# A chunked state-space scan feeding a GELU feed-forward: a new written-out order of all steps, with some steps joined and one mask given a second form

## The chip, the cores and the metric

The kernel runs on one core of one Trainium2 chip. The metric is the device time of one execution in microseconds (us). Three timed executions of the kernel before took 120.58, 120.76 and 121.44 us, so its median is 120.76 us. A further execution was recorded by the hardware profiler; all rows that are quoted come from it.

A core has five engines with a queue each: TensorE (PE; its loads of stationary operands are shown apart as PEld), VectorE (DVE), ScalarE (ACT), GpSimd (POOL) and SyncE (SP, which here only issues transfers). Each engine works through its own queue in the order in which the program issued the instructions, and waits where an operand is not ready.

## What is computed

The reference, cut to what matters. Four batches of eight heads go through a scan in chunks; its result, 3072 tokens of 256, goes through two matrices with a GELU between them.

```python
log_a = np.log(np.clip(a, 1e-06, 1.0))            # x (4,8,768,32), a (4,8,768), B and C (4,8,768,16)
for c in range(nc):
    cum = np.cumsum(la, axis=-1)
    L = np.exp(cum[:, :, :, None] - cum[:, :, None, :]) * causal
    M = np.einsum('bhin,bhjn->bhij', Cc, Bc) * L
    y_intra = np.einsum('bhij,bhjd->bhid', M, xc)
    y_inter = np.einsum('bhin,bhnd->bhid', Cc, state) * np.exp(cum)[:, :, :, None]
    y[:, :, sl] = y_intra + y_inter
    Bx = np.einsum('bhjn,bhjd->bhjnd', Bc, xc) * decay_from_j[:, :, :, None, None]
    state = decay_full[:, :, None, None] * state + np.sum(Bx, axis=2)
x = y.transpose(0, 2, 1, 3).reshape(3072, 256)
h = x @ w_in                                      # 256 x 2048
g = 0.5 * h * (1.0 + np.tanh(c * (h + 0.044715 * h * h * h)))
out = g @ w_out                                   # 2048 x 256
```

## The kernel before, in words

**Tiling.** The kernel uses chunks of 128 time steps, 6 per batch, 24 in all. Two neighbouring chunks are a unit `u`, so there are 12 units of 256 tokens. The eight heads lie side by side on the 128 partitions (16 states each) or in eight groups of 32 columns.

**A list of steps.** The program is cut into named steps (`add`, L722), each a function `f_...` or `c_...` with an engine, the steps it depends on, and the buffers it takes. The string `ORDERED` (L17) names each step once, and the last loop (L895) calls them in that order; so the string alone sets the order of instructions in each engine's queue. A letter behind a colon puts a step on another of the engines that it allows (`:A` ACT, `:D` DVE, `:P` POOL, `:S` SP). `~60` issues 60 blocks of 128 columns of filler matmuls on zeros (`fill`, L672, up to four blocks to an instruction), and `+5` behind an s1 step issues 5 such blocks ahead of it. The tile framework adds the waits that the data demands; it doesn't reorder.

**The scan of a unit.** The steps that the text names are these:

- `load_aq`, `load_a`, `load_bc0`, `load_bc1`, `load_x4`, `load_x`, `load_bc`, `load_wi`, `load_wo`: transfers. `aq` is what the first four chunks need of `a`, `a` is everything of it in two halves. `bc0` brings B (`.0`) and C (`.1`) of chunks 0 to 3 of batch 0, `bc1` of chunks 4 and 5. `x4` is x of chunks 0 to 3. `wi` and `wo` are four blocks each of the two matrices.
- `c_ident`, `c_tri`, `c_cz`, `c_bmask`, `c_m8`: constants made on POOL. `c_bmask` (L232) makes the mask that keeps each head's own block, out of a memset and two affine selects. `c_par` reads it.
- `clipq`, `Rq`, `tpq`, `recip0`: decays of chunks 0 to 3 on DVE; `clip` (L325), `R` (the long scan at L328), `tp2`, `recip1`, `tp6`, `recip`, `pe`: those of all others. `tp2` and `tp6` are transposes on DVE (L339).
- `mulb`, `mulc`, `mul1`, `mul`: B and C times decays on DVE. `tw`, `T1`, `T`: their transposes on PE into PSUM. `ew`, `bh1`, `ce1`, `E`, `F`: the copies out to `bh` and `ce`. `N1`, `N` transpose `bh` back, `bn1`, `bn` copy that out.
- `XX`, `XD`, `xn`: x of the first two units, re-ordered on PE with the products for their states. `castx` does it for later units by a cast.
- `G` (Gram): C times B for both chunks of a unit on PE, in rows of 32, into the PSUM tiles `ga` and `gb`. `M.u.0` and `M.u.1` mask them on DVE (1.2 us each). In unit 0, `GE` and `ME` do half of this by ACT and POOL.
- `D`: the unit's products for the state, on PE, into one of the two PSUM buffers named `hp`. `S` adds them to the state, `SP` makes the masked state for the next chunk; both are on DVE.
- `Y`: the output of both chunks on PE into the PSUM tile `yb`, out of `M`, x and `SP`. `yev` copies it to `xm`.

**The feed-forward of a unit.** `s1.u.i` (L688, eight per unit) multiplies `xm` with two blocks of `w_in` into an `hp` buffer; `gelu.u.i` on ACT (L692) takes it out into `gT`. `s2.u.k.q` (L706) multiplies `gT` with `w_out`, `oev` copies the result out and `store` writes it. `wi.q.k` and `wo.q.k` cast the matrices to bf16 after their loads, on POOL, ACT or DVE. There are two `hp` buffers, shared by `s1`, `D` and a few early steps, and one each of `ga`, `gb` and the output bank.

**The order around the start, before.** On DVE: ... `mulb`, `mulc.0`, `mulc.1`, `peq`, `clip`, two copies, `c_par`, `R`, `M.0.0`, `SP.0`, `S.0.0`, `tp2`, `S.0.1`, `recip1`, `S.1.0`, `mul1.1`, `SP.1`, `M.1.1`, `M.1.0`. On PE: fillers, `tw.0`, `tw.1`, `tw.2`, `G.0`, `XX.0`, `XD.0`, eleven blocks of filler, `Y.0`, `XX.1`, `XD.1`, `s1.0.0`, `G.1` and so on. From unit 3 on the order before has, on PE, `D.3 G.4`, `D.4 Y.3`, `Y.4 D.5 G.5`, `G.6 D.6 Y.5 D.7`, `G.7 D.8 Y.6`, `Y.7 G.8`, `G.9 Y.8 D.9`, `G.10 D.10 Y.9`, `D.11 Y.10 G.11` and `Y.11`, each between s1 and s2 steps.

Of the kernel before, what the change touches and what calls it, by code (L numbers as in the profile page):

```python
# [30 lines left out]
castx.3.None load_x.4 T.1.0 s1.2.1 E.1.0 load_bc.2.1 s2.0.0.2.o E.1.1:A s1.2.2 gelu.2.1 N.1 F.1
castx.4.None gelu.2.2 bn.1:D wo.3.1:D load_bc.2.0 s2.0.1.2.o load_x.5 s1.2.3 wo.3.0:A G.3 M.3.0
s1.2.4 load_bc.3.1 gelu.2.3 load_x.6 s1.2.5 gelu.2.4 s2.0.0.3.o gelu.2.5 s1.2.6 s2.0.1.3.o
gelu.2.6 load_x.7 M.3.1 s1.2.7 D.3 oev.1 S.3.0 oev.0 G.4 gelu.2.7 SP.6 S.3.1 s2.1.0.0.o D.4
castx.7.None Y.3 s2.1.0.1.o s2.1.0.2.o yev.3.0.2 s2.1.0.3.o s1.3.0 S.4.0 M.4.0 S.4.1 M.4.1 mul.2.1
oev.2 s1.3.1 mul.2.0 gelu.3.0 s2.1.1.0.o s2.1.1.1.o gelu.3.1 s1.3.2 load_bc.3.0 s2.1.1.2.o
s2.1.1.3.o gelu.3.2 T.2.1 s1.3.3 SP.8 T.2.0 gelu.3.3 s1.3.4 oev.3:D load_x.8 castx.5.None:A E.2.0
s2.2.0.0.o SP.9 s2.2.0.1.o gelu.3.4 s1.3.5 N.2 s1.3.6 bn.2 E.2.1 s2.2.0.2.o SP.7 gelu.3.5 gelu.3.6
s2.2.0.3.o Y.4 castx.6.None:D yev.4.0.2 D.5 oev.4:D G.5 S.5.0 store.2 s1.3.7 s1.4.0 gelu.3.7
gelu.4.0 s2.2.1.0.o s1.4.1 gelu.4.1 s2.2.1.1.o M.5.0 SP.10 s2.2.1.2.o s1.4.2 s2.2.1.3.o s1.4.3  # L40
gelu.4.2 s1.4.4 M.5.1 gelu.4.3 F.2 G.6 oev.5:D D.6 S.6.0 Y.5 gelu.4.4 S.6.1 D.7 S.7.0 s2.3.0.0.o
# [24 lines left out]
store.19 s2.10.1.0.o s2.11.0.0.yb s1.11.5 s2.10.1.1.o s2.11.0.1.yb store.16 gelu.11.5 s1.11.6  # L66
s2.10.1.2.o gelu.11.6 store.20 s1.11.7 store.15 store.18 s2.10.1.3.o gelu.11.7 oev.21 s2.11.0.2.yb
store.21 s2.11.0.3.yb s2.11.1.0.o s2.11.1.1.o s2.11.1.2.o s2.11.1.3.o oev.22 store.22 oev.23
store.23
# [864 lines left out]
```

## Time and profile before

| what | value |
|---|---|
| timed executions | 120.58, 120.76, 121.44 us |
| the profiled execution | 121.85 us, of which 120.1 us from its first to its last instruction |
| mean granted clock of PE | 0.971 of full speed |
| PE busy | 113.1 us, 94% of the span |
| DVE busy | 74.5 us, 62% |
| ACT busy | 73.0 us, 61% |
| POOL busy | 16.2 us, 14% |
| moved by DMA | 14.00 MB |
| s1 matmuls (L688), 384 | 54.7 us, 277 ns each |
| s2 matmuls (L706), 352 and 32 | 47.4 and 4.5 us, 273 ns each |
| GELU (L692), 96 | 54.2 us, 597 ns each |

A matmul's 277 ns are its length from start to end; neighbours overlap, and four of them start within 0.437 us at the full clock. The page shows the span in 40 slices of 3 us with the busy share of each engine in tenths. "PEclk" is the clock that PE was granted. In rows of the timeline the numbers are the start, the length (of a whole group, if it stands for several instructions), the engine, the line, the operation, what is written and read, the shape and the number; in brackets stands how long the engine was idle just before and what ended that.

Chain of waits that ended last, shares of the span: PE 87%, DMA 7%, ACT 2%, DVE 1%.

### The profile page before, as it was taken

The numbers are of one execution on the slowest core, as the hardware profiler recorded it, in microseconds if no ns is written. First come the engines' busy times: TensorE is split into PE (matmuls) and PEld (weight loads), VectorE is DVE, ScalarE is ACT, GpSimd is POOL, SyncE is SP. The second block draws the span as 40 slices with busy tenths as digits, with TensorE's granted clock in tenths as the row PEclk, the third lists the DMA queues.
The fourth block names the chain that finished last, engine by engine and source line by source line (L and its number), as shares of the span: only waits on it lengthen the run. The fifth ranks groups of instructions, "written<-read, shape, count | busy, mean of one in ns | idle before, by whom it ended". The sixth has DMA issues, their size and how long they took to land.

```text
span 120.1 us, 3430 instructions
## 1 busy us (share of the span) xinstructions
PE 113.1 (94%) x1456; PEld 94.1 (78%) x1456; DVE 74.5 (62%) x147; ACT 73.0 (61%) x142; POOL 16.2 (14%) x33
## 2 busy tenths in 40 slices
PE   6948999999999999999999999999999999999990
PEld 2324457888887998989799979888989899999970
DVE  6289799999979977969597356798645003102000
ACT  2227649966974658668665574543786565576430
POOL 7315776205300020020000000000000000000000
PEclk9997559999999999999999999999999999999999
DMA  3999989996949877900400060006100001001521
GB/s 70 223 294 278 371 216 270 359 247 102 271 76 215 174 136 159 196 8 0 132 5 0 0 124 13 5 6 212 49 27 17 0 5 44 0 5 46 175 87 44
DMA packets 37662, 14.00 MB, mean 117 GB/s; under 512 B 31824, under 2 KB 36112, under 8 KB 37648
## 3 DMA queue, kind: packets, MB, share of 16 engines
q1 hardware_dynamic: 37456, 13.70, 44.5%
q8 instruction: 11, 0.18, 0.6%
q10 hardware_dynamic: 192, 0.10, 0.4%
q14 instruction: 3, 0.02, 0.1%
HBM read 10.65 MB, written 3.15 MB: 115 GB/s over the span
## 4 chain that ended last, share of the span: by engine, by line
PE 87%; DMA 7%; ACT 2%; DVE 1%; issue 0%; ACTq 0%
PE hp L688 36%; PE o_ps L706 32%; DMA a_t<-in_a_dram 5%; PE ga L574 3%; PE yb L706 3%; PE yb L629 3%; PE yb L638 2%; DMA aq_t<-in_a_dram 2%; ACT gT L692 1%; PE yb L676 1%; PE hp L607 1%; PE ga L500 1%; PE gb L481 1%; PE ga L481 1%; PE hp L542 1%; DVE bh L315 1%
## 5 line engine op out<-in xcount | busy, mean ns | idle before, releaser
L692 ACT ACTIVATE gT<-hp 128x512 bf16<-128x512 f32 x96 | 54.2, 597 | 28.0 <-PE hp L688 27.6
L688 PE MATMUL hp<-xm,w_in_sb 128*128 128x256 bf16 x384 | 54.7, 277 | 0.2 <-ACT gT L692 0.2
L706 PE MATMUL o_ps<-w_out_sb,gT 128*128 128x256 bf16 x352 | 47.4, 273 | 0.0
L688 PEld LDWEIGHTS <-w_in_sb 128*128 128x128 bf16 x384 | 41.1, 114 | 3.7 <-issue 1.7
L706 PEld LDWEIGHTS <-gT 128*128 128x128 bf16 x384 | 37.1, 98 | 4.1 <-issue 0.2
L315 DVE COPY o_sb<-o_ps 128x256 f32<-128x256 f32 x9 | 3.8, 425 | 20.5 <-PE o_ps L706 20.3
L584 DVE TENSOR_TENSOR m<-ga,tri 128x1024 bf16<-128x1024 f32 x12 | 14.6, 1217 | 0.7 <-PE gb L574 0.6
L584 DVE TENSOR_TENSOR m<-gb,tri 128x1024 bf16<-128x1024 f32 x11 | 13.4, 1220 | 0.9 <-PE gb L574 0.9
L313 POOL CAST x<-x_t 128x512 bf16<-128x512 f32 x5 | 4.5, 893 | 27.4 <-DMA x_t<-in_x_dram 27.4
L662 DVE SCALAR_TENSOR_TENSOR sp_new<-s_new,pend,bmask 128x256 bf16<-128x256 f32 x17 | 8.0, 473 | 0.0
L676 PE MATMUL yb<-wz 128*128 128x512 bf16 (+2 forms) x20 | 6.8, 489 | 1.1 <-DVE warm L219 1.1
L311 ACT ACTIVATE o_sb<-o_ps 128x256 f32<-128x256 f32 x13 | 4.8, 381 | 4.7 <-PE o_ps L706 4.7
L638 PE MATMUL yb<-m,x 128*32 128x128 bf16 x192 | 6.4, 226 | 0.0
L655 DVE SCALAR_TENSOR_TENSOR s_new<-s_new,pend,hp 128x64 f32<-128x64 f32 x13 | 3.6, 279 | 4.5 <-PE hp L607 4.1
L311 ACT ACTIVATE xm<-yb 128x512 bf16<-128x512 f32 x7 | 4.2, 598 | 2.4 <-PE yb L638 2.0
L676 PEld LDWEIGHTS <-wz 128*128 128x128 bf16 x20 | 2.2, 119 | 4.2 <-issue 2.4
L629 PE MATMUL yb<-ce,sp_new 128*32 128x128 bf16 x160 | 5.4, 225 | 0.0
L574 PE MATMUL ga<-ce,bh 32*128 32x256 bf16 x48 | 4.9, 283 | 0.3 <-ACT ce L311 0.3
L574 PE MATMUL gb<-ce,bh 32*128 32x256 bf16 x48 | 4.9, 284 | 0.0
L638 PEld LDWEIGHTS <-x 128*32 128x32 bf16 x192 | 3.9, 100 | 0.7 <-ACT x L311 0.7
L706 PE MATMUL yb<-w_out_sb,gT 128*128 128x256 bf16 x32 | 4.5, 273 | 0.0
L315 DVE COPY bh<-ga 128x768 bf16<-128x768 bf16 (+1 forms) x4 | 3.3, 824 | 1.5 <-PE ga L481 1.3
(110 smaller groups left out, 87.7 us busy)
## 6 DMA issues: line engine op xcount, KB each, us to landing
out_dram<-o_sb SPq DMA_DIRECT2D x24, 128.0 KB, 1.8
x_t<-in_x_dram SPq DMA_DIRECT2D x20, 128.0 KB, 4.1
...
```

Source lines behind the costliest of these rows:

```text
L311: nc.scalar.activation(o, i, AF.Copy)
L313: nc.gpsimd.tensor_copy(out=o, in_=i)
L315: nc.vector.tensor_copy(out=o, in_=i)
L574: nc.tensor.matmul(out=gbank(g)[:, 256 * k:256 * k + 256], lhsT=bh_of(2 * u + k)[gs], rhs=ce_of(2 * u + k)[gs], start=True, stop=True, til ...
L584: nc.vector.tensor_tensor(out=m_of(u)[:, 2 * i:2 * i + 2].rearrange("p g k e t -> p (g k e) t"), in0=gx[i].rearrange("p g (k t) -> p (g k) ...
L629: nc.tensor.matmul(out=y4[32 * j:32 * j + 32, k, w], lhsT=sp[:, 32 * h:32 * h + 32], rhs=ce_of(gc)[:, h % 2], start=first(j), stop=False, ...
L638: nc.tensor.matmul(out=y4[32 * j:32 * j + 32, k, w], lhsT=X16[u][:, k, 32 * h:32 * h + 32], rhs=m[:, h // 2, h % 2, :], start=first(j), st ...
L662: nc.vector.scalar_tensor_tensor(out=sp_new.rearrange("p (g d) -> p g d", g=4), in0=(XN[0][:, H * D:H * D + 64] if gc == 0 else state[("s" ...
L676: nc.tensor.matmul(out=t[:, 0:m * 128], lhsT=wz, rhs=w3.to_broadcast([128, m, 128]), start=True, stop=True, skip_group_check=True)
L688: nc.tensor.matmul(out=hp[:, j * T:(j + 1) * T], lhsT=w_in_k[:, w, q, k], rhs=xm[:, w, u * T:(u + 1) * T], start=(w == 0), stop=(w == 1))
L692: nc.scalar.activation(gts[u][:, 2 * i:2 * i + 2], hps.pop((u, i)).rearrange("p (j t) -> p j t", j=2), AF.Gelu_apprx_tanh)
L706: nc.tensor.matmul(out=ops[gc], lhsT=gts[u][:, fi, k * Q:(k + 1) * Q], rhs=w_out_sb[:, fi, :], start=(fi == 0 and (u > 0 or k == 0)), stop ...
```

## The change

The change has four parts.

1. `ORDERED` is written anew. All steps of before are in it but those of part 2. Around the start: DVE does `mulc.0`, `mulc.1` ahead of `mulb`, and PE `tw.1`, `tw.2` ahead of `tw.0`; `R` stands behind `S.0.0`, and `tp2`, `pe`, `mul1.0`, `recip1`, `mul1.1` behind `SP.2`. `load_a.0` goes to ACT's queue, `load_aq.3` instead of `load_aq.2` to SP's. The four `load_wi` follow `load_x4` directly, and `load_bc1.1` and `load_bc1.0` come behind them. `xn.0`, `wi.3.0` and both `ce1` go to DVE; `bh1` and `bn1` go to ACT. The fillers are `~59`, `~4`, `~2`, `~1`, `~17` instead of `~60`, `~4`, `~2`, `~11`, and `s1.1.5`, `s1.2.0` and `s1.2.1` get 1, 5 and 6 blocks ahead of them.
2. For units 3 to 10, `Y.u`, `D.(u+1)` and `G.(u+1)` become one step that issues the three in this order, with the dependencies and buffers of all of them.
3. `c_bmask` depends on `c_ident` and gets a second form for DVE (a reduction of the identity and a broadcast copy), which runs if its entry in the order ends in `:D`. The new order has `c_bmask` without a letter.
4. A constant tile `sel16` for that form.

The diff, with the order's string cut to its first lines. Later lines hold the same kinds of steps.

```diff
 ORDERED = """
-load_bc0.1 c_wz load_aq.0 c_ident c_zero c_cz load_aq.1 load_aq.2:S c_unp load_bc0.0 load_aq.3
-c_m4 c_sel clipq c_tri Rq tpq recip0 mulb mulc.0 load_x4 mulc.1 c_warm load_a.0 ~60 tw.0 tw.1
-load_a.1:A peq ew.0.0:A load_wi.0 c_bmask tw.2 clip ew.0.1:A load_bc1.1 ew.0.2:A ew.1.2:A
-load_wi.1 ~4 G.0 ew.1.0 x4.1 ew.1.1 GE.3 ~2 ppq x4.0:P c_par XX.0 R M.0.0 ME.3 pendq GE.2 XD.0
-ME.2 xn.0 SP.0 xn.1 wi.0.1:A ~11 Y.0 c_m8 S.0.0 tp2 wi.0.0 S.0.1 XX.1 recip1 XD.1 yev.0.0.2
-wi.1.1:A S.1.0 s1.0.0 wi.1.0 load_wi.2 xn.2 wi.2.0 mul1.1 SP.1 gelu.0.0 load_wi.3 G.1 s1.0.1
-wi.2.1 s1.0.2 wi.3.0 load_bc1.0 gelu.0.1 load_wo.0 gelu.0.2 s1.0.3 M.1.1 M.1.0 xn.3 tp6.3 s1.0.4
-load_x.2 T1.1 gelu.0.3 SP.2 pe mul1.0 s1.0.5 load_wo.1 gelu.0.4 wi.3.1 s1.0.6 Y.1 tp6.0 wo.0.0
-gelu.0.5 gelu.0.6 pp wo.0.1 tp6.2 s1.0.7 load_bc.1.1 yev.1.0.2 S.1.1 pend T1.0 load_bc.1.0 bh1:D
-castx.2.None ce1.1 s1.1.0 gelu.0.7 N1 load_wo.2 gelu.1.0 wo.1.0 ce1.0 s1.1.1 tp6.1 bn1:D s1.1.2
-s2.0.0.0.o gelu.1.1 gelu.1.2 D.2 recip.1.4 load_wo.3 SP.3 S.2.0 G.2 wo.1.1 M.2.0 s1.1.3 SP.4
-s1.1.4 s2.0.1.0.o M.2.1 mul.1.1 gelu.1.3 s1.1.5 gelu.1.4 s2.0.0.1.o gelu.1.5 s1.1.6 gelu.1.6
-mul.1.0 s1.1.7 load_x.3 Y.2 yev.2.0.2 s2.0.1.1.o wo.2.1:D T.1.1 wo.2.0:D gelu.1.7 s1.2.0 gelu.2.0
...
+c_wz load_bc0.1 load_aq.0 c_ident c_m4 c_sel load_aq.2 c_tri load_aq.3:S c_zero load_bc0.0
+load_aq.1 c_unp load_a.0:A clipq load_x4 Rq tpq recip0 c_cz mulc.0 ~59 tw.1 load_wi.0 c_warm
+load_a.1:A ew.1.1:A mulc.1 c_bmask tw.2 mulb ~4 tw.0 peq ew.0.2:A clip ew.0.1 load_wi.1 ew.0.0:A
+ew.1.2 c_par ~2 G.0 x4.1 ew.1.0 M.0.0 ~1 ppq GE.2 pendq x4.0:P XX.0 ME.2 XD.0 GE.3 xn.1 ME.3
+xn.0:D load_wi.2 SP.0 ~17 Y.0 wi.0.1:A wi.0.0:A S.0.0 yev.0.0.2 wi.1.1 XX.1 wi.1.0:A R XD.1 S.0.1
+load_wi.3 S.1.0 s1.0.0 SP.1 xn.2 load_bc1.1 c_m8 wi.2.0 gelu.0.0 G.1 s1.0.1 s1.0.2 M.1.1 M.1.0
+load_bc1.0 load_wo.0 wi.3.0:D gelu.0.1 wi.2.1 s1.0.3 load_x.2 load_wo.1 SP.2 tp2 load_bc.1.1
+gelu.0.2 s1.0.4 gelu.0.3 gelu.0.4 pe load_bc.1.0 mul1.0 wi.3.1 recip1 xn.3 tp6.2 s1.0.5 load_wo.2
+mul1.1 wo.0.1 s1.0.6 gelu.0.5 Y.1 s1.0.7 load_wo.3 gelu.0.6 yev.1.0.2 T1.0 s1.1.0 wo.0.0 tp6.1
+gelu.0.7 castx.2.None s1.1.1 bh1 wo.1.1 N1 T1.1 gelu.1.0 gelu.1.1 s1.1.2 tp6.0 bn1 ce1.1:D
+load_x.3 gelu.1.2 load_x.4 s1.1.3 ce1.0:D G.2 pp gelu.1.3 pend s1.1.4 gelu.1.4 S.1.1 tp6.3 wo.3.1
+s1.1.5+1 gelu.1.5 s2.0.0.0.o wo.1.0:A s1.1.6 M.2.0 load_bc.2.1 D.2 SP.3 M.2.1 S.2.0 s2.0.1.0.o
+SP.4 s2.0.0.1.o recip.1.4 gelu.1.6 mul.1.1 s1.1.7 mul.1.0 gelu.1.7 wo.2.0:D Y.2 yev.2.0.2
+castx.3.None s2.0.1.1.o s1.2.0+5 gelu.2.0 s1.2.1+6 wo.2.1:D T.1.1 gelu.2.1 E.1.1:A T.1.0 s1.2.2
+E.1.0 s1.2.3 N.1 F.1 bn.1:D wo.3.0:D gelu.2.2 s1.2.4 load_bc.2.0 s2.0.0.2.o gelu.2.3 gelu.2.4 G.3
...
 """
...
+    sel16 = const.tile([128, H], BF16, name="sel16")
...
-    def c_bmask():
+    def c_bmask(eng):
+        if eng == "DVE":
+            with nc.allow_low_precision("sums of one 1 and zeros"):
+                nc.vector.tensor_reduce(out=sel16, in_=ident.rearrange("p (h n) -> p h n", n=N), op=ALU.add,
+                                        axis=mybir.AxisListType.X)
+            nc.vector.tensor_copy(out=bmask.rearrange("p (h d) -> p h d", d=D),
+                                  in_=sel16.rearrange("p (h o) -> p h o", o=1).to_broadcast([128, H, D]))
+            return
         nc.gpsimd.memset(bmask, 1.0)
...
-    ccz, cid, ctri, cbm, cm8 = (add("P", f) for f in (c_cz, c_ident, c_tri, c_bmask, c_m8))
+    ccz, cid, ctri, cm8 = (add("P", f) for f in (c_cz, c_ident, c_tri, c_m8))
+    cbm = add("P", c_bmask, alt="PD", deps=[cid])
...
+    for u in range(3, NU - 1):
+        y = steps[f"Y.{u}"]
+        gone = [steps.pop(f"D.{u + 1}"), steps.pop(f"G.{u + 1}")]
+        y.fn = lambda fs=(y.fn, gone[0].fn, gone[1].fn): [f() for f in fs]
+        for d in gone:
+            y.deps += d.deps
+            y.allocs += d.allocs
+        for z in steps.values():
+            z.deps = [y if d in gone else d for d in z.deps]
+            z.allocs = [(p, [y if d in gone else d for d in by]) for p, by in z.allocs]
+        y.deps = [d for d in y.deps if d is not y]
```

More of the change, by code (lines that the diff above doesn't have):

```diff
@@ L30 @@
-mul.1.0 s1.1.7 load_x.3 Y.2 yev.2.0.2 s2.0.1.1.o wo.2.1:D T.1.1 wo.2.0:D gelu.1.7 s1.2.0 gelu.2.0
[L31 to L41, printed above, removed]
@@ L66 @@
[L66 to L69, printed above, removed]
+c_wz load_bc0.1 load_aq.0 c_ident c_m4 c_sel load_aq.2 c_tri load_aq.3:S c_zero load_bc0.0
+load_aq.1 c_unp load_a.0:A clipq load_x4 Rq tpq recip0 c_cz mulc.0 ~59 tw.1 load_wi.0 c_warm
+load_a.1:A ew.1.1:A mulc.1 c_bmask tw.2 mulb ~4 tw.0 peq ew.0.2:A clip ew.0.1 load_wi.1 ew.0.0:A
@@ new lines @@
+store.13 s1.9.0 store.12 s1.9.1 gelu.9.0 s2.7.1.0.o s2.7.1.1.o s2.7.1.2.o Y.10 store.11 s2.7.1.3.o
+store.14 S.11.0 gelu.9.1 s1.9.2 s1.9.3 oev.15:D s2.8.0.0.o s2.8.0.1.o s2.8.0.2.o s2.8.0.3.o
+gelu.9.2 oev.16:D M.11.0 yev.10.0.2 s1.9.4 gelu.9.3 s1.9.5 gelu.9.4 s2.8.1.0.o s2.8.1.1.o
+s2.8.1.2.o gelu.9.5 s1.9.6 s2.8.1.3.o M.11.1 s1.9.7 gelu.9.6 s1.10.0 gelu.10.0 oev.17:D s2.9.0.0.o
+s2.9.0.1.o s2.9.0.2.o SP.22 gelu.9.7 s1.10.1 gelu.10.1 s1.10.2 gelu.10.2 Y.11 s1.10.3 gelu.10.3
+s2.9.0.3.o s1.10.4 store.16 store.15 s1.10.5 gelu.10.4 yev.11.0.2:D store.17 gelu.10.5
```

54 lines of the change are left out of this document (30 added, 24 removed).

## The prediction

> **What bounds the kernel now.** I read the page's slices first, then busy time by stretch, then the instructions of DVE and PE in order of time between 8 and 33 us, and last the chain of waits. The page, slices of 3 us:
>
> ```profile
> PE   6948999999999999999999999999999999999990
> DVE  6289799999979977969597356798645003102000
> PEclk9997559999999999999999999999999999999999
> ```
>
> PE is full from the fifth slice to the end, and its granted clock is halved in slices 5 and 6. Asked in finer stretches, the clock is 0.66 in 10.7 to 10.8 us, 0.50 after it, 0.71 in 17.5 to 17.6: a low stage of 6.8 us. Busy time by stretch (PE, PEld, DVE, ACT, POOL, then clock, DMA share, GB/s):
>
> ```profile
> 10.00:15.00 5.00, 4.84 (x110) 2.48 (x111) 4.16 (x13) 3.43 (x8) 3.57 (x8) 0.57 1.04 343
> 15.00:20.00 5.00, 4.79 (x35) 3.06 (x36) 4.64 (x8) 3.40 (x7) 3.86 (x7) 0.74 0.88 228
> 25.00:30.00 5.00, 5.00 (x80) 4.55 (x78) 5.00 (x7) 3.50 (x7) 1.54 (x1) 1.00 0.74 130
> 60.00:80.00 20.00, 20.00 (x263) 18.06 (x262) 14.12 (x20) 10.89 (x21) 0.00 (x0) 1.00 0.12 22
> ```
>
> From 25 to 30 us DVE is as full as PE. From 60 us on PE alone is, so the end is: the moment at which PE stops waiting for DVE, plus PE's remaining matmuls. Where that moment lies shows in DVE's own instructions (start, length, what it is, idle before it):
>
> ```profile
> 10.16 0.94 DVE L328 TENSOR_TENSOR_SCAN r_t<-ac,ends 64x384 f32<-64x384 f32 x1
> ...
> 12.81 0.98 DVE L339 STREAM_TRANSPOSE rt<-r_t 32x64 f32<-32x64 f32 x4
> ...
> 14.02 0.25 DVE L371 RECIPROCAL pt<-rt 128x16 f32<-128x16 f32 x1
> 15.10 0.28 DVE L655 SCALAR_TENSOR_TENSOR s_new<-s_new,pendq,hp 128x64 f32<-128x64 f32 x1 [0.83 <-PE hp L552]
> ...
> 16.57 1.23 DVE L584 TENSOR_TENSOR m<-gb,tri 128x1024 bf16<-128x1024 f32 x1 [0.20 <-PE gb L574]
> ...
> 22.18 0.42 DVE L315 COPY bh<-ga 128x256 bf16<-128x256 bf16 x1 [0.19 <-PE ga L440]
> ...
> 23.19 0.29 DVE L315 COPY bn<-ga 128x256 bf16<-128x256 bf16 x1
> ...
> 30.20 0.96 DVE L315 COPY bh<-ga 128x768 bf16<-128x768 bf16 x1 [0.20 <-PE ga L481]
> ...
> 32.12 0.54 DVE L315 COPY bn<-ga 128x768 bf16<-128x768 bf16 x1
> ```
>
> and in PE's:
>
> ```profile
> 11.57 1.35 PE L676 MATMUL yb<-wz 128*128 128x512 bf16 x3
> 12.85 0.40 PE L638 MATMUL yb<-m,x 128*32 128x128 bf16 x8
> ...
> 14.92 1.05 PE L688 MATMUL hp<-xm,w_in_sb 128*128 128x256 bf16 x4
> ...
> 32.72 0.28 PE L574 MATMUL ga<-ce,bh 32*128 32x256 bf16 x2
> ```
>
> From S.1.0 at 15.10 to the end of bn.1 at 32.66 DVE works 17.56 us and idles 0.20 + 0.19 + 0.20 in it. G.3 on PE starts 0.06 after bn.1 lets go of ga, and the step before it (32.08) takes 0.63 to the next start where its kind takes 0.53 in front of 32-row matmuls. So this DVE run of 17.56 us is what PE last waits for. Everything behind G.3 is paid in PE time.
>
> **The change, part by part.**
>
> *Y with D and G.* In the merged stretches Y.3 to Y.10 each carry the next D and G. In the trace Y.4, D.5, G.5 already stand together:
>
> ```profile
> 46.31 0.30 PE L629 MATMUL yb<-ce,sp_new 128*32 128x128 bf16 x8
> ...
> 46.91 0.28 PE L574 MATMUL ga<-ce,bh 32*128 32x256 bf16 x2
> ...
> 47.23 1.06 PE L688 MATMUL hp<-xm,w_in_sb 128*128 128x256 bf16 x8
> ```
>
> Entering such a stretch costs 0.09 (0.53 instead of 0.437 between starts), leaving it 0.03. Before, from D.3 on, there are ten stretches, adding up to 9.07 us; after, also ten (D.3 alone, nine with a Y), 9.10 by the same rows. D.2 and G.2, one stretch before, become two: +0.1, early, where PE waits anyhow. So merging buys about nothing: +0.03.
>
> *The mask.* The new VectorE form of c_bmask is not taken (its entry has no D behind it). Its three GpSimd instructions move behind the clearing of cz and end near 4.1 us; par needs them at 9.3. Zero; without that cover 0.2.
>
> *Loads.* SP issues w_in 0 to 3 directly behind x4; chunks 4 and 5 (128 KB each) follow. Half of a goes from SP's queue to ACT's, where the other half landed at 6.7 us. The 0.38 that DVE waits at L325 for a should go; the second half now waits on ACT's queue for an aq load, in which case clip keeps the 0.38. w_in 1 to 3 come sooner (their casts on POOL now wait 0.74 and 0.27 for them); the C of chunks 4 and 5 comes later than its 10.5 (issued 5.37, 5.1 to landing), but hardly after 16.3, where their B lands now (8.38 + 7.9), since the same bytes are ahead of both; DVE wants them after 21. PE waits for gT and DVE in this stage, not for w_in: zero.
>
> *The first steps on DVE.* The scan R (0.94 at 10.16) goes behind S.0.0. M.0.0 starts near 9.9 instead of 11.03. G.0 starts when ce's copy on DVE is out: 8.52 (clip) + 0.46 + 0.41 = 9.39, so 9.43 against 9.25. ppq no longer waits until 10.10, XX.0 starts at 10.15 (x4's second half on ACT), XD.0 is out near 11.0 instead of 11.57. Then come 17 filler blocks instead of 11. Eleven took 1.28 (12.85 - 11.57); 17 at the low clock are four matmuls of 0.43, one block of 0.11 and 0.1 of change-over: 1.92. Y.0 starts at 12.9, as before. At full clock they take 0.96 and Y.0 starts at 12.1, when the second masked copy on GpSimd is out (11.25 + 0.80); before, at full clock, SP.0 on DVE holds Y.0's second half until 12.7.
>
> *What is put behind S.1.0.* tp2 (12.81 to 13.82) and recip1 filled DVE's wait for XD.1; now they stand behind SP.2. Between S.1.0 and bn.1 DVE gains, start to start: tp2 1.01, recip1 0.20, w_in's cast wi.3.0 0.38 (the w_out cast of the same shape takes 0.41), two ce1 0.68 (nearest: the copies of 128x256 out of PSUM on DVE, 0.41 long, 0.34 start to start; ends 0.21 as bn1 and 0.48 as ACT's own ce1). It loses bh1 0.46 and bn1 0.21. Net 1.60, from 1.34 to 1.88. The added x copy xn.0 (0.4) lies ahead of S.1.0, where DVE waits.
>
> *The sum.* Low clock as in the profile: XD.1 ends with the same Y.0, S.1.0 at 15.10. M.1.1 waits for G.1 0.59 longer, since mul1.1 (15.30 to 15.89) no longer stands ahead of it; the waits of 0.19 and 0.20 vanish under the queue. 17.56 + 1.60 + 0.59 - 0.39 = 19.36, bn.1 ends at 34.46 instead of 32.66: +1.80. Full clock throughout: S.1.0 at 13.45 (Y.0 12.1, out by 12.6, half of 0.96 + 0.34 for XX.1 and XD.1) against 14.22 before, where tp2 and recip1 hold it. After: 13.45 + 17.56 - 0.59 + 0.15 + 1.60 = 32.2; before: 14.22 + 17.56 - 0.20 = 31.6, or 31.2 if its waits for PE go too. +0.6 to +1.0, take +0.8. Before G.3 PE has issued equally many L688 and L706 steps in both, so this difference goes to the end. The 12 new filler blocks in s1.1.5, s1.2.0 and s1.2.1 (0.66 at 0.055 each) lie in PE's wait for yev.2 and for T.1 and N.1, and cost nothing extra while DVE is late; if it isn't, 0.66.
>
> The profiled execution took 121.85 (span 120.1, 1.75 around it), 1.09 over the median. Both columns may occur in the timed runs, so I take the middle, +1.3, on the median: 120.76 + 1.3 = 122.1. On the profiled execution itself, with its low stage, it would be 123.6.
>
> The Trainium skill, "TensorE: Matmul & The Clock Gate", in "Why this matters for your kernels", says that the clock drops after PE gaps of more than about 3 us. Here the longest gap ahead of the drop is 1.85 us (5.86 to 7.71), so the trace disagrees; by that rule the full-clock column would hold for both kernels, and the time would be 121.6. Part 1 of that page calls the activity window free-running at 3.4 us; the low stage of 6.8 us is two of these, and by that rule it may fall elsewhere in another execution.
>
> **Rivals.** *No change:* the new DVE work comes out at its low ends (ce1 at 0.21, 1.34 net) at full clock, and S.1.0 0.2 earlier than 13.45: 0.6 - 0.26 - 0.2, +0.2 with the pauses left, 121.0. For it: DVE's wait of 1.9 us ahead of S.1.0 in the low-clock column looks wasteful and would shrink. Against: DVE at 5.00 of 5.00.
>
> *Faster:* the clock. XX.0 starts 0.3 sooner and PE's pauses before it are shorter; if that keeps the clock full where it now falls, s1.0.0 starts at 13.35 instead of 14.92. This decides only if DVE also passes bn.1 by about 31.2, 1.0 sooner than I add up, because then PE's start sets the end: 120.76 - 1.5 = 119.3. For it: PE loses some 1.2 us to the low clock in 14.92 to 17.3 alone. Against: DVE's row above.
>
> *Stretches that hold hp:* each D now takes one of two hp buffers inside the stretch until its two S are done. With S behind an M (1.2), one s1 must wait for gelu (0.60) each time: 0.3 in eight stretches, 2.4: 123.2. Against: S waits for D now (4.1 us in four waits), not D's buffer for S.
>
> **Numbers.** Forecast (the DVE run grows) 0.54, no change 0.22, faster 0.17, hp 0.07. The forecast's own range is 121.4 to 122.9. A change of 1%, 1.2 us, is what can be told: faster than 119.55, slower than 121.97. Slower: two thirds of the forecast, 0.36, and hp 0.07: 0.43. Faster: 0.15 of the faster rival. Same: the remaining 0.42. Low end 120.3 leaves out the faster rival; high end 123.2 takes in the low-clock sum with ce1 at its high end (0.28) and the hp case's near end.
>
> **What would show it.** Right: S.1.0 by 13.5 to 15.1, DVE without pause from there to bn.1, bn.1 ending 1 us or more later, G.3 right behind it, then PE without gaps. DVE idle about 1.9 us ahead of S.1.0 shows the low-clock column. Wrong: clock 1.00 in slices 5 and 6 with G.3 before 31.5; or L688 waiting for s_new after 40 us.

## The result, and the profile after

| | timed executions, us | median | ratio to before, 95% interval |
|---|---|---|---|
| before | 120.58, 120.58, 120.76, 121.44 | 120.67 | |
| after | 126.06, 126.40, 127.88, 128.27 | 127.14 | 1.0491 [1.0379, 1.0604] |

The change makes the kernel slower by some 6 us, where 1.3 had been forecast and 123.2 was the top of the range. (The intervals, here and below, leave out executions that lie more than 1.5% above a kernel's fastest, so a ratio needn't be the quotient of the medians.) The profiled execution after took 126.06 us with a span of 124.1. It is the fastest of the four; that of before, 121.85, was the slowest of its own. So the two profiles lie 4.2 us apart, and the other 2.3 of the 6.5 us lie between them and the medians.

A part of that is the clock. The mean granted clock of each execution of after is on record: 0.946 to 0.973 in all four. The profile of before had 0.971, but of 71 further executions of before, timed beside the experiments, 64 had 0.995 or more (median 120.5 us) and only seven 0.958 to 0.972 (median 121.5 us). The profile of before thus shows the rarer case, which costs that kernel about 1 us.

The page's slices of after, now 3.1 us each:

```profile
PE   6972999989999999999999999999999999999990
...
DVE  5584959999999789979945492669400182201100
...
PEclk9999657999999999999999999999999999999999
```

PE has a hole in the fourth slice, and the low stage of the clock stands one slice later than before. Asked in stretches (length of the stretch, then busy time of PE, PEld, DVE, ACT, POOL, then clock, DMA share, GB/s), the hole shows in the first line and the full DVE from 25 to 30 us in the third:

```profile
10.00:15.00 5.00, 3.39 (x76) 1.85 (x79) 4.07 (x10) 2.69 (x7) 2.18 (x5) 0.86 1.02 274
15.00:20.00 5.00, 5.00 (x77) 2.66 (x66) 3.72 (x6) 2.69 (x5) 3.91 (x8) 0.50 0.89 229
25.00:30.00 5.00, 4.49 (x48) 3.53 (x46) 4.92 (x9) 3.99 (x10) 1.22 (x2) 1.00 0.92 166
60.00:80.00 20.00, 20.00 (x268) 18.09 (x266) 11.93 (x22) 13.08 (x25) 0.00 (x0) 1.00 0.30 69
```

What PE waits for in the hole is the first copy of C on DVE (start, length, what it is, idle before it):

```profile
8.75 0.27 PE L683 MATMUL yb<-wz 128*128 128x256 bf16 x1
11.61 0.28 PE L581 MATMUL ga<-ce,bh 32*128 32x256 bf16 x2 [2.59 <-DVE ce L322]
...
13.06 1.55 PE L683 MATMUL yb<-wz 128*128 128x512 bf16 x5
...
36.78 0.28 PE L581 MATMUL ga<-ce,bh 32*128 32x256 bf16 x2
```

and DVE itself waits for `a`. In these rows of DVE the first is `clip` and the second the copy `ce` that PE waits for; then come `R`, `S.1.0`, `SP.1` and, at the end of the run, `bn.1`:

```profile
10.87 0.35 DVE L332 TENSOR_SCALAR ac<-a_t 64x384 f32<-64x384 f32 x1 [1.93 <-DMA a_t<-in_a_dram]
11.15 0.41 DVE L322 COPY ce<-hp 128x256 bf16<-128x256 bf16 x1
...
14.17 1.17 DVE L335 TENSOR_TENSOR_SCAN r_t<-ac,ends 64x384 f32<-64x384 f32 x1
...
16.79 0.28 DVE L662 SCALAR_TENSOR_TENSOR s_new<-s_new,pendq,hp 128x64 f32<-128x64 f32 x1 [1.28 <-PE hp L559]
16.99 1.65 DVE L669 SCALAR_TENSOR_TENSOR sp_new<-s_new,pendq,bmask 128x256 bf16<-128x256 f32 x1
...
36.01 0.56 DVE L322 COPY bn<-ga 128x768 bf16<-128x768 bf16 x1
```

ACT's issues show why `a` is late. Its second half is asked for in the last row; before, one half went out on ACT's queue at 2.45 us and the other on SP's at 3.45:

```profile
2.37 0.59 ACTq L158 DMA_DIRECT2D a_t<-in_a_dram  x1
2.99 1.28 ACT L227 ACT_TABLE_LOAD   x1 [2.99 <-issue]
4.28 0.20 ACT L227 ACTIVATE warm<-warm 128x1 f32<-128x1 f32 x1
5.30 0.34 ACTq L158 DMA_DIRECT2D a_t<-in_a_dram  x1
```

The issue at 5.30 waits for a semaphore that the third small `aq` load gives back when it lands, at 5.28. By then SP has begun to ask for w_in (from 3.35 us on, four blocks of 512 KB). The half lands at 10.85 us, behind w_in's first block (9.37) and just ahead of its second (11.24): 5.55 us after its issue, for 48 KB.

From here on one number serves as a gauge: the start of G.3 on PE. From there to the end of PE's last matmul pass 84.20 us before (32.72 to 116.92) and 84.17 after (36.78 to 120.95). All that the change costs between these two executions, 4.06 us, lies ahead of G.3.

It comes in three parts. S.1.0 starts 1.69 us later (15.10 to 16.79). From there to G.2 pass 0.78 us more (9.28 to 10.06; SP.1 alone is 1.18 longer). From G.2 to G.3 pass 1.59 us more (8.34 to 9.93). In that last stretch PE is as full as DVE, before (first line) and after (second):

```profile
24.38:32.72 8.34, 8.31 (x119) 7.38 (x116) 8.10 (x15) 6.34 (x12) 2.62 (x2) 1.00 0.86 196
26.85:36.78 9.93, 9.75 (x125) 7.96 (x126) 9.80 (x17) 6.79 (x14) 2.48 (x4) 1.00 1.06 172
```

By the profile PE pauses for 0.03 us in it before and for 0.18 after. Most of the 1.59 is work that the new order puts there. These are PE's rows of it in after: `pp` (a small product out of `pe`), D.2, which like `pp` stood ahead of G.2 before, and the 12 new blocks of filler (`wz`):

```profile
27.18 0.40 PE L397 MATMUL hp<-pe,selp 64*128 64x24 f32 x2
27.97 0.22 PE L683 MATMUL hp<-wz 128*128 128x128 bf16 x1
29.43 0.21 PE L614 MATMUL hp<-x,bn 128*32 128x64 bf16 x4
32.00 0.43 PE L683 MATMUL hp<-wz 128*128 128x512 bf16 x2
32.76 0.49 PE L683 MATMUL hp<-wz 128*128 128x512 bf16 x2
```

From their start to the start of what follows they take 0.33 (`pp`), 0.15 (D.2) and 0.7 us (filler), together 1.2.

### The profile page after: what moved, and what is told of

It is laid out like the page before. It is cut to its first block, busy times and chain, and to the rows that moved or that the text cites. A ratio compares the mean times of both kernels' runs of the same rounds, so it can differ in the third digit from the quotient of the medians.

```text
span 124.1 us, 3445 instructions
## 1 busy us (share of the span) xinstructions
PE 116.0 (93%) x1464; PEld 95.1 (77%) x1464; DVE 75.4 (61%) x146; ACT 74.0 (60%) x144; POOL 15.2 (12%) x32
## 4 chain that ended last, share of the span: by engine, by line
PE 73%; DVE 15%; DMA 7%; issue 1%; ACTq 1%; ACT 0%; DVEq 0%
PE o_ps L713 30%; PE hp L695 27%; DMA a_t<-in_a_dram 4%; DVE m L591 4%; PE yb L713 3%; DMA aq_t<-in_a_dram 3%; PE ga L581 3%; DVE rt L346 2%; PE yb L645 2%; DVE sp_new L669 2%; PE yb L636 2%; DVE bc L479 1%; PE yb L683 1%; PE ga L507 1%; DVE pt L386 1%
## 5 line engine op out<-in xcount | busy, mean ns | idle before, releaser
L683 PE MATMUL yb<-wz 128*128 128x512 bf16 (+3 forms) x23 | 8.6, 529 | 1.1 <-DVE wz L216 1.1
L683 PEld LDWEIGHTS <-wz 128*128 128x128 bf16 x28 | 3.4, 126 | 5.4 <-issue 4.1
L318 ACT ACTIVATE xm<-yb 128x512 bf16<-128x512 f32 x8 | 4.8, 596 | 0.8 <-PE yb L645 0.7
L581 PEld LDWEIGHTS <-bh 32*128 32x128 bf16 x96 | 1.5, 93 | 4.6 <-issue 2.8
L322 DVE CAST xm<-yb 128x512 bf16<-128x512 f32 x4 | 2.7, 687 | 2.8 <-ACT gT L699 2.8
```

Of the source, the lines that this page charges most:

```text
L318: nc.scalar.activation(o, i, AF.Copy)
L322: nc.vector.tensor_copy(out=o, in_=i)
L581: nc.tensor.matmul(out=gbank(g)[:, 256 * k:256 * k + 256], lhsT=bh_of(2 * u + k)[gs], rhs=ce_of(2 * u + k)[gs], start=True, stop=True, til ...
L683: nc.tensor.matmul(out=t[:, 0:m * 128], lhsT=wz, rhs=w3.to_broadcast([128, m, 128]), start=True, stop=True, skip_group_check=True)
```

## The experiments

Seventeen kernels. "Before" in each row is the kernel before, timed beside it on the same chip. G.3 is from the one profiled execution; L marks those whose clock was at half for a stretch (6.8 us unless the text says another length).

| run | what | median, us | ratio, 95% interval | G.3 at |
|---|---|---|---|---|
| 1 | after, half of `a` on SP | 122.64 | 1.0194 [1.0144, 1.0245] | 33.22 |
| 2 | after, tp2 and recip1 early | 127.23 | 1.056 [1.0506, 1.0614] | 38.50 L |
| 3 | 1 and 2 | 122.79 | 1.0206 [1.0163, 1.0249] | 33.16 |
| 4 | before, with Y, D, G joined | 121.82 | 1.0089 [1.0055, 1.0123] | 32.35 L |
| 5 | before, half of `a` behind w_in 0 | 122.52 | 1.0122 [1.0078, 1.0165] | 34.38 L |
| 6 | after, half of `a` earlier on ACT | 122.64 | 1.0171 [1.0115, 1.0228] | 34.43 L |
| 7 | 3, DVE relieved, first try | 128.32 | 1.0631 [1.0568, 1.0694] | 38.68 L |
| 8 | before, two casts to POOL | 120.65 | 0.9987 [0.9958, 1.0017] | 31.56 |
| 9 | 1, DVE relieved | 122.73 | 1.0206 [1.0143, 1.0269] | 33.04 |
| 10 | before, with after's DVE work | 123.56 | 1.026 [1.0177, 1.0343] | 34.46 L |
| 11 | before, w_in in a row | 120.94 | 1.0043 [1.0003, 1.0082] | 31.30 |
| 12 | before, both halves of `a` early | 119.13 | 0.99 [0.9845, 0.9954] | 30.31 |
| 13 | 9, recip.1.4 early | 122.12 | 1.0144 [1.0076, 1.0211] | 32.64 |
| 14 | 1, recip.1.4 early | 122.44 | 1.0172 [1.0112, 1.0233] | 33.07 |
| 15 | 12 and 8 | 119.08 | 0.9887 [0.983, 0.9945] | 29.94 |
| 16 | 13, T.1 early | 122.04 | 1.0104 [1.0064, 1.0144] | 32.41 |
| 17 | before, T.1 late | 121.46 | 1.0068 [1.0034, 1.0102] | 32.16 |

In the short diffs, lines are pieces of the order's string.

### The late half of `a`, and tp2: runs 1, 2 and 3

Run 1 gives SP's queue one half of `a` back, behind `x4`, and puts the other where it doesn't wait:

```diff
 load_aq.1 c_unp
-load_a.0:A
+load_a.1:A
 clipq load_x4
+load_a.0
 Rq tpq
...
 load_wi.0 c_warm
-load_a.1:A
 ew.1.1:A mulc.1
```

> The changed kernel with the two halves of a loaded as before: one on ACT's queue in fourth place, where it waits for no lane, the other on SP behind x4. Theory 'late load': in the changed kernel DVE's clip (L332) waits 1.93 us for the second half, which lands at 10.85, and everything behind it on DVE starts that much later. Then both halves land by 8.9, S.1.0 starts near 15.1 instead of 16.8, and the time falls by 1.7 or a little more, from 127.1 to 125.4 or less. Rival 'the load only uncovers another wait' (w_in casts, x4): S.1.0 moves by less than 0.5 and the time stays above 126.5. If all of the loss were this load, the time would be that of before, 120.7.

Run 2 leaves the loads and puts tp2 and recip1 ahead of S.1.0 again; run 3 does both.

```diff
 wi.1.0:A R
+tp2
 XD.1 S.0.1
+recip1
 load_wi.3 S.1.0
...
 load_wo.1 SP.2
-tp2
...
 mul1.0 wi.3.1
-recip1
```

> The changed kernel with tp2 and recip1 back ahead of S.1.0, where DVE idles 1.28 us in the changed kernel. Theory 'longer DVE run': from S.1.0 to bn.1 DVE now takes 19.8 us (17.6 before), 1.2 of the difference is tp2 and recip1; the run falls to 18.6 and the time by 1.2, to 125.9. Rival 'PE or ACT sets this stage': the run shortens but G.3 does not move, 127.1.

> Both edits together. If the two causes add up: 1.7 + 1.2 less than the changed kernel, 124.2; G.3 on PE near 33.9 instead of 36.8. If one hides the other: no better than the better of the two alone.

Measured: 122.64, 127.23 and 122.79 us. Run 1 takes back 4.5 of the 6.5 us. tp2's place is worth nothing with `a` in time (run 3 against run 1); with `a` late, run 2 and after differ by less than the executions of either do. `clip` in run 1 and in run 2 (rows of DVE):

```profile
8.68 0.34 DVE L331 TENSOR_SCALAR ac<-a_t 64x384 f32<-64x384 f32 x1
```

```profile
12.44 0.35 DVE L331 TENSOR_SCALAR ac<-a_t 64x384 f32<-64x384 f32 x1 [4.06 <-DMA a_t<-in_a_dram]
```

In run 1 `a` is there (8.23 us) before DVE is, and nothing waits. Run 2 has the changed kernel's loads, unaltered, and there `clip` waited 4.06 us where it waited 1.93 in the profile of after: the late half lands at another moment in each execution. That fits the spread of after's executions (126.06 to 128.27), and that 4.5 us come back where its profile, taken of the shortest, showed a wait of 1.93. Between the two profiles `clip` is 2.19 us earlier (10.87 to 8.68) and G.3 3.56 (36.78 to 33.22). The 1.37 between these are no more than an estimate of what the low stage of the clock costs PE there; run 1's profile has no such stage.

So the 4.5 us are not the wait alone. All eight executions of after and run 2 had a granted clock of 0.946 to 0.973, while of the 34 in which the new order had `a` in time (runs 1, 3, 6, 9, 13, 14 and 16) 32 had 0.995 or more. By what the low stage costs the kernel before, about 1 of the 4.5 us is the clock's; this is an estimate, since no run parts the two.

### Is it the queue or the moment? Runs 5 and 6

Run 5 gives the kernel before a late half alone, on SP behind w_in's first block. Run 6 leaves the changed kernel's half on ACT and asks for it earlier.

```diff
 mulc.1 c_warm
-load_a.0
 ~60 tw.0 tw.1
-load_a.1:A
+load_a.0:A
 peq ew.0.0:A load_wi.0
+load_a.1
```

> The kernel before with one half of a asked for behind w_in's first block on SP's queue and the other half alone on ACT's; nothing else moves. Theory (the late half of a is what cost the changed kernel most of its time): the half lands at 10 to 11 us instead of 8.88, clip waits 1.5 to 2.5 us where it waited 0.38, and the first D, S.1.0 and the end of the DVE run move with it: about 122.5 us against 120.5, and up to 124 if the low stage of the clock moves too. Rival (the late half hurt only because the changed order has a longer DVE run behind it, and the order of before can absorb it): no change, 120.5 us.

```diff
 clipq load_x4
+load_a.1:A
 Rq tpq
...
 load_wi.0 c_warm
-load_a.1:A
```

> The changed kernel with one step moved: the second half of a is asked for right behind x's first load instead of behind w_in's first block and the table load, still on ACT's queue. Theory (it is the time of the issue that counts, not the queue): both halves land by about 8 us, clip does not wait, and the time is that of the kernel with one half on SP, 122.6 us. Rival (ACT's queue itself is the trouble, four small loads and two halves of a in a row): the half lands late again, 124 to 127 us.

Measured: 122.52 and 122.64 us. In run 5 the half landed at 9.68 us, later by 0.80 than before, `clip` waited 1.07 us, and the time grew by 1.2% (1.9 us between the medians). It isn't the new order that makes the late half dear. Nine of run 5's ten executions had a granted clock of 0.958 to 0.972, against two of the 19 of before beside it, and the edit moved nothing but the loads of `a`: so the late half brings the low stage along. About half of the 1.9 us is the clock's, as the one execution at full clock took 121.07 us, 0.5 more than before at that clock. Why the clock falls then, the traces don't show. In run 6 both halves landed by 6.38 us and the time is run 1's: the moment of the issue counts, not the queue. (In run 6's profile G.3 is late all the same: that execution, at 123.71 us the slowest of its four, had the low stage, and x landed at 9.27 us, in run 1 at 8.01.)

### Both halves early: runs 12, 8 and 15

Run 12 turns this round, in the kernel before: both halves on ACT's queue ahead of the table load.

```diff
 load_bc0.0 load_aq.3
+load_a.0:A load_a.1:A
 c_m4 c_sel
...
 mulc.1 c_warm
-load_a.0
 ~60 tw.0 tw.1
-load_a.1:A
 peq
```

> The kernel before with both halves of a in a row on ACT's queue ahead of the table load, so that they land by about 6.5 us instead of 6.9 and 8.9; x's first load then waits for a lane and goes out about 1 us later. Theory (DVE's chain from clip to S.1.0 starts at the landing of a, and clip waited 0.38 us for it): 0.2 to 0.4 us faster, 120.3 us. Rival (x takes a's place as the last to land): 120.6 to 121.5 us.

Measured: 119.13 us, 1.0% faster than before. The gain of 1.3 us is more than the 0.2 to 0.4 that were expected of `clip`'s wait. Its row of DVE:

```profile
7.76 0.34 DVE L324 TENSOR_SCALAR ac<-a_t 64x384 f32<-64x384 f32 x1
```

`clip` starts 1.14 us earlier than before (8.90), 0.38 of it by its own wait, the rest because what stands ahead of it on DVE is earlier too. Against run 8, whose loads are those of before and whose clock is full, S.1.0 starts 0.62 earlier (12.85 to 13.47), G.2 1.78 (21.34 to 23.12) and G.3 1.25 (30.31 to 31.56). A part of what is won between S.1.0 and G.2 is `pe`: its two instructions take 0.56 and 0.47 us in run 8, where casts run on POOL beside them, and 0.15 and 0.17 here. The rest wasn't taken apart.

Run 8 takes two casts of w_out's third block from DVE to POOL in the kernel before, run 15 the same on top of run 12.

```diff
 s1.1.3 SP.4
+wo.2.0 wo.2.1
 s1.1.4 s2.0.1.0.o
...
 yev.2.0.2 s2.0.1.1.o
-wo.2.1:D
 T.1.1
-wo.2.0:D
 gelu.1.7
```

> The kernel before with two casts of w_out's third block (0.43 us each by its trace) taken from DVE's run to POOL. Theory (the same DVE run sets the start of G.3 in the kernel before): G.3 starts about 0.7 us earlier and the time falls from 120.5 to about 119.8 us. Rival (the run has no weight in the kernel before): 120.5 us. It would be slower, 121 us, if casts on POOL lengthen the DVE instructions beside them by as much as they take away.

> The kernel before with both halves of a early on ACT's queue (119.13 us) and the two casts of w_out's third block taken from DVE to POOL, behind the second block's: in that run's trace DVE waited 0.62 us for that block and then held bh of chunk 1 back, from about 27.3 us, when T.1.0 ended, to 27.99. Theory: bh and G.3 start 0.7 us earlier and the time is about 118.4 us. Rival (PE waits for the same block in s2.0.0.2, a step further on, and that sets G.3): 119.1 us, or more as POOL's cast takes 0.61 us for 0.38.

Measured: 120.65 (no change) and 119.08 us (against run 12's 119.13 no change that can be told). In run 8 the casts' place on DVE turned into a wait for T.1.0 on PE: 0.68 us ahead of `bh` of chunk 1, where the trace of before has 0.20. In run 15 G.3 came 0.37 us earlier, half of what was expected, and the timed executions don't show it.

### Joining, and w_in in a row: runs 4 and 11

Run 4 gives the kernel before the loop that joins Y, D and G, and no more of the new order than that needs: S.6.0, S.7.0, S.7.1, SP.14, SP.15 and S.8.0 go behind the Y that now holds their D.

```diff
+    for u in range(3, NU - 1):
+        y = steps[f"Y.{u}"]
+        gone = [steps.pop(f"D.{u + 1}"), steps.pop(f"G.{u + 1}")]
+        y.fn = lambda fs=(y.fn, gone[0].fn, gone[1].fn): [f() for f in fs]
...
```

> The kernel before with only Y, D and G joined for units 3 to 10 (and the S steps of three units moved behind them, as they must be). Mine: a stretch costs 0.09 to enter and 0.03 to leave, and there are about as many as before, so 120.7 within 0.3. Rival 'D holds one of two hp buffers': an s1 waits for gelu once in each of eight stretches, 0.3 each, 123.1. Rival 'joining saves stretches': 119.8.

Run 11 moves the load of C's chunks 4 and 5 behind w_in's four blocks, in the kernel before.

```diff
 clip ew.0.1:A
-load_bc1.1
 ew.0.2:A ew.1.2:A
...
 xn.2 wi.2.0
-mul1.1
 SP.1 gelu.0.0 load_wi.3
+load_bc1.1 mul1.1
```

> The kernel before with w_in's four blocks in a row on SP's queue: the load of C's chunks 4 and 5 (bc1.1) goes from between blocks 0 and 1 to behind block 3, and mul1.1, which reads it, two steps down. The forecast costed this at nothing, and theory says so again: 120.6 us. Rival (block 1 comes about 0.5 us earlier and s1.0.2 or the casts waited for it): 120.1 us. Rival on the other side (mul1.1 now waits for its load in DVE's run): 121.2 us.

Measured: 121.82 and 120.94 us. Run 11 is 0.4% slower (0.03% to 0.8%), so near the forecast's zero; the gain of the first rival is excluded. In run 4 PE takes 85.32 us from G.3 (32.35) to its last matmul (117.67), where before takes 84.20: joining, with the S and SP steps that had to move, costs 1.1 us in an order that wasn't made for it, mostly in two pauses ahead of Y.9 (s1.7.6 0.66 and s2.6.1.0 0.99 us to the next start, where 0.437 is usual). The new order has none of that (84.17).

### The other two microseconds: runs 7, 9, 10, 13, 14, 16 and 17

With `a` in time DVE works from S.1.0 (13.36) to the end of bn.1 (33.02) for 19.66 us. Run 7 was to shorten that run, and went wrong:

```diff
-wi.3.0:D
+wi.3.0
...
 s1.0.7 load_wo.3
+wo.2.0 wo.2.1
 gelu.0.6 yev.1.0.2
...
-ce1.1:D
+ce1.1
...
-ce1.0:D
+ce1.0
...
-wo.2.0:D
...
-wo.2.1:D
```

> The changed kernel with both repairs (a's half on SP, tp2 and recip1 early) and five DVE steps of its run taken to other engines: two casts of w_out's third block and one of w_in's fourth to POOL, two copies to ACT. Theory (with a in time, what is left of the loss is the DVE run from S.1.0 to bn.1): the run is shorter by the five steps, 1.7 us, and the time falls from 122.8 to about 121.0 us. Rival (PE's own work and the chain of the recurrence set the end of that stage, DVE only follows): no change, 122.8 us.

Measured: 128.32 us, and nothing said of the theory. On POOL the two casts stood ahead of the second block's cast and of the cast of x's chunk 2, and waited there until 27.12 us for the third block's load; PE waited 3.41 us for a weight, and Y.2 started at 32.96 us, in run 3 at 26.58. Run 9 is the same relief on top of run 1, with these casts behind the casts of x:

```diff
 yev.2.0.2 castx.3.None
+wo.2.0 wo.2.1
 s2.0.1.1.o
```

> The changed kernel with a's half on SP (as in the first experiment, 122.64 us), and besides: ce1.1 and ce1.0 from DVE to ACT, wi.3.0 from DVE to POOL, and wo.2.0 and wo.2.1 from DVE to POOL, this time behind the casts of chunks 2 and 3 there, which in the run before last but one had to wait behind them. By its trace DVE's run from S.1.0 to the end of bn.1 loses 0.42 + 0.82 + 0.75 = 1.99 us of 19.66. Theory (that run is what is left of the loss): G.3 starts at about 31.3 us instead of 33.22 and the time is about 120.7 us, level with the kernel before. Rival (the order of the steps on PE sets that stage): 122.6 us, with DVE waiting for PE where it was busy.

Measured: 122.73 us, no change, as the rival had it. Most of the 1.99 us that left DVE came back as waits (rows of DVE: the mask M.2.0, and `bh` of chunk 1):

```profile
23.25 1.23 DVE L590 TENSOR_TENSOR m<-ga,tri 128x1024 bf16<-128x1024 f32 x1 [1.13 <-PE gb L580]
...
30.55 0.96 DVE L321 COPY bh<-ga 128x768 bf16<-128x768 bf16 x1 [0.60 <-PE ga L487]
```

G.2 itself starts at 22.74 us, in run 8 at 23.12: up to G.2 this order is not behind. From G.2 to G.3 pass 10.30 us, in run 8 8.44. PE works almost without a pause there in both (by the profile busy for 9.94 of 10.30 us and 8.30 of 8.44), and the 1.2 us of `pp`, D.2 and filler are in run 9 too: relieving DVE doesn't touch them. Two more differences in this stretch were tried: recip.1.4 (1.05 us) stands behind M.2.0, M.2.1 and SP.4 on DVE instead of ahead of them, and T.1.1 and T.1.0 stand behind s1.2.1 and the two last groups of filler on PE. Runs 13 (from run 9) and 14 (from run 1) move the first:

```diff
 S.1.1 tp6.3
+recip.1.4
 wo.3.1
...
 SP.4 s2.0.0.1.o
-recip.1.4
```

> The changed kernel with a in time and DVE relieved of 1.99 us (the run of 122.73 us), and besides recip.1.4 (1.05 us) taken from behind SP.4 to ahead of M.2.0, where DVE stood idle for 1.13 us in that run, waiting for G.2. Theory (between G.2 and G.3 a chain binds, M.2.0 to recip.1.4 to the two products of chunk 1 to T.1 to bn.1, and recip.1.4 is its one link that need not be in it): G.2 stays at 22.7 us, G.3 comes 1.05 us earlier, at about 32.0 us, and the time is 121.6 to 121.7 us. Rival (PE's order after G.2, with s1.1.4 to s2.0.0.2 ahead of G.3, fills that stretch): 122.7 us.

> The changed kernel with a in time (122.64 us) and recip.1.4 taken from behind SP.4 to ahead of M.2.0, without the relief. Theory (DVE is busy without a gap ahead of M.2.0 here, so the 1.05 us only changes sides): G.3 where it was, at 33.2 us, and 122.6 us. Rival (the place of recip.1.4 is a loss by itself, for M.2.0 is not on the path): about 121.6 us.

Measured: 122.12 and 122.44 us; G.3 at 32.64 and 33.07. Alone the move gains next to nothing (G.3 0.15), with the relief 0.6 us in the time and 0.40 at G.3, less than the 1.05 expected; the intervals of the ratios overlap in both cases. What came in its place shows in run 13's rows, first DVE's two products and `bh` of chunk 1, then PE's T.1.1 and T.1.0 behind s1.2.1:

```profile
27.52 0.95 DVE L478 TENSOR_TENSOR bc<-bc_t,rt 128x768 bf16<-128x768 f32 x1
30.31 0.96 DVE L321 COPY bh<-ga 128x768 bf16<-128x768 bf16 x1 [1.85 <-PE ga L487]
```

```profile
28.68 0.49 PE L682 MATMUL hp<-wz 128*128 128x512 bf16 x2
29.00 0.60 PE L694 MATMUL hp<-xm,w_in_sb 128*128 128x256 bf16 x4
29.44 0.50 PE L487 MATMUL gb<-ident,bc 128*128 128x128 bf16 x6
29.78 0.50 PE L487 MATMUL ga<-ident,bc 128*128 128x128 bf16 x6
```

The products are ready at 28.47, but PE does fillers and an s1 step first. Run 16 takes that out of run 13, run 17 puts it into the kernel before. With T.1 go the 11 blocks of filler ahead of s1.2.0 and s1.2.1.

```diff
 s2.0.1.1.o
-s1.2.0+5 gelu.2.0 s1.2.1+6 T.1.1 gelu.2.1 E.1.1:A T.1.0
+T.1.1 E.1.1:A T.1.0 s1.2.0 gelu.2.0 s1.2.1 gelu.2.1
 s1.2.2
```

> The run of 122.12 us (the changed kernel with a in time, DVE relieved, recip.1.4 early) and besides T.1.1, its copy E.1.1 and T.1.0 directly behind s2.0.1.1, as near as in the kernel before, and the fillers ahead of s1.2.0 and s1.2.1 (5 and 6 matmuls, 0.65 us) left out. In that run DVE had the products of chunk 1 ready at 28.47 us, T.1.1 started at 29.44, and DVE then stood idle for 1.85 us. Theory (PE's order holds T.1 back, the last link of the 2.0 us): T.1.1 at 28.5 us, bh of chunk 1 at 29.2 instead of 30.31, G.3 about 1.0 us earlier, 121.1 us. Rival (PE has as much work ahead of G.3 either way, and DVE has the slack): 122.1 us, or 121.5 for the fillers alone.

```diff
-T.1.1
 wo.2.0:D gelu.1.7
-s1.2.0
+s1.2.0+5
 gelu.2.0 castx.3.None load_x.4
+s1.2.1+6 T.1.1
 T.1.0
-s1.2.1
```

> The kernel before with only that place of the changed order: T.1.1 and T.1.0 behind s1.2.1, with the fillers of 5 and 6 matmuls ahead of s1.2.0 and s1.2.1. Theory: T.1.0 starts 1.1 us later and bh, bn.1 and G.3 with it: 121.5 us against 120.4. Rival (DVE's casts, which stand between the products and bh, hide it): 120.4 to 120.6 us.

Measured: ratios of 1.0104 and 1.0068. In run 16 `bh` started at 29.07, 1.24 us earlier, but G.3 only 0.23 (32.41): `ce` and bn.1 now waited for ACT and PE. The filler that left had taken 0.64 us of PE; PE's pauses from G.2 to G.3 grew from 0.18 to 0.40 us instead. The time (0.08 us between the medians) doesn't show the step. In run 17 G.3 was at 32.16 and the time 0.7% longer (0.3% to 1.0%, so 0.4 to 1.2 us, with the 1.1 expected inside). From G.2 to G.3 it takes 9.29 us, 0.85 more than run 8, and 0.64 of that is the filler itself. So run 17 doesn't show that T.1's place is dear. Run 10, last, puts the changed kernel's additions to DVE into the kernel before:

```diff
 S.0.0
-tp2
...
-recip1
...
-mul1.1
...
-wi.3.0
+wi.3.0:D
...
-T1.1
...
 SP.2
+tp2
 pe
+recip1 mul1.1
...
 pp wo.0.1
+T1.1
...
-bh1:D
+bh1
...
-ce1.1
+ce1.1:D
...
-ce1.0
+ce1.0:D
...
-bn1:D
+bn1
```

> The kernel before with only the changed kernel's additions to DVE's run: tp2 and recip1 behind SP.2 (1.23 us, off the path ahead of S.1.0), wi.3.0 from POOL to DVE (0.42 us), ce1.1 and ce1.0 to DVE for bh1 and bn1 to ACT (0.82 for 0.71 us); mul1.1 and T1.1 follow recip1. Loads as before. Theory: the run is longer by 1.76 us, S.1.0 no more than 0.1 us earlier, and the time 1.6 to 1.8 us longer, 122.3 us against 120.6. Rival (the run has slack in the kernel before, as it showed none of the gain when two casts left it): 120.6 us.

Measured: 123.56 us, 2.6% slower, more than the 1.7 us by which DVE's run was to grow. All four executions had a granted clock of 0.972 or 0.986 and none of the 13 of before beside them less than 0.995, so a part of this is the clock's; and PE waited 1.2 us for `pe` in the profile. So DVE's additions cost time in an order that isn't made for them, how much by themselves is not shown, and in the new order taking them away alone gives nothing. As `a` was loaded as before, a late half isn't the only thing that brings the low stage. The rows of runs 9, 13 and 16 suggest why: PE is nearly full too, and each edit opens a wait that stood ready behind the last one, for `ce1` on ACT ahead of G.2, for T.1 on PE, and for ACT and PE ahead of bn.1.

## Why the prediction was wrong, and where it was right

**The step that failed** is this one: "The 0.38 that DVE waits at L325 for a should go; the second half now waits on ACT's queue for an aq load, in which case clip keeps the 0.38." The wait for an `aq` load was seen. What was mis-sized is what follows it. An issue at 5.30 us was given a landing near that of before (8.88). It landed at 10.85 and, in run 2, 12.41, since it now stood behind w_in's blocks in the DMA engines. A term of 0 to 0.38 us was 1.93 to 4.06 us at `clip` and 4.5 us in the time (run 1, the clock's share included), and nothing covers it: `clip` stands ahead of C's first copy on DVE, and PE's G.0 waits for that.

**The clock, the second step that failed.** The forecast set like against like, low with low (+1.80) and full with full (+0.8), and took the middle. What was timed was mostly before at the full clock against after always at the low one. By the forecast's own figures that is bn.1 at 34.46 against 31.2 to 31.6, some 3 us instead of 1.3. That both columns occur was right (7 of the 19 profiles have the low stage near the start); that the change decides which of them occurs was not foreseen, and run 5 shows the late half doing so.

**The head, otherwise right.** Forecast with `a` in time and the full clock, measured in run 1: G.0 9.43 and 9.41; M.0.0 9.9 and 9.84; Y.0 12.1 and 11.88; S.1.0 13.45 and 13.36 us.

**DVE's run: it grew, by more than was added up, and it isn't the bound alone.** In after it took 19.78 us from S.1.0 to bn.1 where 19.36 had been added up. That this is near is luck in part: the wait of 0.59 for G.1 was not there, and SP.1 took 1.65 us for 0.47. In run 1 it took 19.66 for 18.72, so bn.1 ended at 33.02 and not 32.2, and the time was 2.2 us above before's, not 0.8. Three instructions are longer than counted. Rows of run 1:

```profile
18.31 0.52 DVE L388 TENSOR_TENSOR pe<-ac,r_t 64x3 f32<-64x3 f32 x1
...
20.20 0.79 DVE L438 TENSOR_TENSOR bc0s<-bcf,pt 128x256 bf16<-128x256 f32 x1
...
28.94 1.36 DVE L478 TENSOR_TENSOR bc<-bc_t,rt 128x768 bf16<-128x768 f32 x1
```

They take 0.15, 0.42 and 0.95 us where no cast runs on POOL: 1.15 us more. That DVE's run is a sum by which the time goes up and down one for one, though, was too simple: run 9 shows that taking 1.99 us out of it gains nothing. The reading that this run "is what PE last waits for" rested on 0.1 us ahead of G.3; from G.2 to G.3 PE was busy for 8.31 of 8.34 us. The 12 filler blocks were to lie in PE's waits. In after they take 0.7 us of a stretch in which PE pauses for 0.18; taking 11 of them out (run 16) moved G.3 by 0.23 only, as DVE and ACT then are what PE waits for. So several chains end within some tenths of a microsecond of each other there, and the prediction had one.

**The end is G.3 plus PE's work: right.** From G.3 on PE takes 84.20 us before and 84.17 after, and no wait shows on PE after 40 us in either. So joining cost nothing that shows in the new order (+0.03 forecast for it; -0.03 measured for all that lies behind G.3 together), and the rival by which D holds an `hp` buffer falls. Run 4 shows that this doesn't hold in the order before.

**w_in in a row: zero.** Run 11 is 0.4% slower (0.03% to 0.8%), so the term is 0 to 1 us and not below. **tp2's place**: by the forecast's figures it costs DVE's run 1.21 us (with recip1) and, at the full clock, gives 0.77 back at S.1.0. Run 3 against run 1 shows the kind (the run 0.72 shorter, S.1.0 0.66 later), but as good as nothing is left of it: G.3 is 0.06 earlier, and the time shows no difference.

**What stays open.** Of the 2 us that remain with `a` in time, 0.6 at G.3 come back with DVE relieved and recip.1.4 early, and 0.23 more with T.1 early and the filler gone (ratio 1.0104 left). Up to G.2 nothing is lost (22.89 us in run 1, 23.12 in run 8), so the last 1% lies between G.2 and G.3, where `pp` and D.2 still take 0.5 us of PE. No run put these back ahead of G.2, so this stays an argument. Open is also why a late half brings the low stage of the clock.
